# MoBA attention and GELU MLP on one core: batch 0's k sums and gate as fp32 matmuls, the last output row in two pieces, a new order of all steps

## Chip, core and metric

The kernel runs on one core of a Trainium2 chip. A core has five engines with instruction streams of their own: TensorE (PE, matrix products and transposes; its weight loads run beside them as PEld), VectorE (DVE), ScalarE (ACT), GpSimd (POOL) and SyncE (SP, which here only issues DMAs). Sixteen DMA engines move data between HBM and the on-chip memory SBUF. Matrix products write to PSUM, which this kernel uses as eight banks of 512 fp32 columns. The metric is device time in microseconds for one launch, lower is better; the median over several runs counts.

## Reference

q, k and v have the shape (4, 8, 768, 64): 4 batches, 8 heads, 768 tokens, 64 values each. Each token attends causally to its own block of 64 keys and to the three blocks of highest gate score, where a gate score is the product of a query with the mean of the keys of a block. The result, with the heads side by side, is a matrix of 3072 tokens by 512, which goes through an MLP with tanh-GELU (512 to 2048 to 512). All inputs and the output are float32.

```python
    k_rep = k.reshape(B, H, n_blocks, block, D).mean(axis=3)
    gate_scores = np.einsum('bhsd,bhnd->bhsn', q, k_rep)
    ...
    top_idx = np.argsort(gate_scores, axis=-1)[..., -top_k:]
    ...
    mask = mask & (pos[:, None] >= pos[None, :])
    scores = np.where(mask, scores, -1000000000.0)
    ...
    return np.matmul(attn, v).astype(np.float32)
...
    h = x @ w_in
    c = np.float32(np.sqrt(2.0 / np.pi))
    g = 0.5 * h * (1.0 + np.tanh(c * (h + 0.044715 * h * h * h)))
    return (g @ w_out).astype(np.float32)
```

## The kernel before

Nothing is scheduled by the compiler: the kernel gives each small piece of work a name, a step, and a long string ORDER lists all 1113 steps in program order. An engine executes its own instructions in that order and waits on semaphores only for data and for buffers. A step's name ends with `@0`, `@1` or `@2` where it takes one of the three wide PSUM buffers (two banks each), and with `:a`, `:v` or `:p` where it can run on ACT, DVE or POOL. One further PSUM bank belongs to the pool `small` (gates, mask transposes, x transposes, the k sums of later batches) and one to the pool `ops` (results of the down projection, and the filler).

The work has three parts.

*Batch 0* is done in slices, so that something can start before much is loaded. A unit g.c is a group g of four heads and a slice c of 256 tokens; there are six. The letters of its steps: d0 and dd load (L348 to L383), r re-sorts a loaded slice in SBUF (L385), t2 transposes q and k in fp32 on PE into a wide buffer w (L426), h2 makes the fp16 version, scaled by 32 (L445), l the fp16 remainder of q, "low part" (L452), s the sums of k over blocks of 64 (L461), b puts them into the block matrix kb0 as high and low part (L471), v copies v to fp16 (L488), g computes the gate as four fp16 products, high and low part of each side (L495), m selects (L512), mt and mc turn the mask (L542, L551), k computes scores (L565), ma adds the mask on PE (L582), x is the exponential (L603), a the causal cut on POOL (L622), p the product with v (L631), n the normalisation (L646), xt and xc the transposition of the result into xT, the MLP's input (L663, L673).

*Batches 1 to 3* are done in pairs of heads, p = 4 to 15, four pairs for a batch. d loads (L397), hn and ln make high and low fp16 parts (L706, L713), zqh, zkh and zql transpose them by DMA (L723, issued by SP), c0 and c1 copy them into the score operands (L733), and s, b, g, m, mt, mc, k (six bins), x, a, p, n, xt and xc follow as above (L738 to L877).

*The MLP* is done in 12 chunks of 256 tokens. u.ch.dj.half is the up projection, 8 matmuls of 256 columns (L913); dj counts quarters of the 2048 hidden values. y is the GELU of a quarter (L930). f.ch.ti.dj is a quarter of the down projection for 128 tokens, 4 matmuls of 512 columns into an `ops` bank (L938); o copies that bank to SBUF (L950), w stores it (L955). The weights come in eight pieces of 512 KB each for w_in and w_out, loaded by lw (L319) and cast to fp16 by cw (L331).

The constants are steps too (c.*). The steps dmN issue N matmuls of zeros by zeros (L970), whose result nobody reads. All loads go through SP's queue in the order of the list, except that `load_first` issues the k parts from ACT (L356). The SBUF pools that matter: io has 9 buffers for loaded q, k and v, w32 has 7 for raw weights, otp has 2 for output rows.

```python
        dma = nc.scalar if x == 1 else nc.sync
...
    def k_sum0(g, c):
        ks = hd.tile([128, 2, 4], FP32, tag="ks", name=f"ks_{g}_{c}")
...
    for name in ORDER.split():
        do(name)
```

Of the kernel before, what the change touches and what calls it, by code (L numbers as in the profile page):

```python
# [26 lines left out]
d0.0.0.0 d0.0.1.0 d0.0.0.1 c.bd c.e0 c.ident d0.0.1.1 c.e.3:p c.gate dd.0.1.0 dd.0.1.1 d0.1.1.0  # L27
d0.1.0.0 c.e.2:v d0.1.0.1 r.0.1.0:p dm20 t2.0.0@0 r.0.1.1:p d0.1.1.1 c.m0.0 dd.1.1.0 d0.0.1.2
c.m0.1 c.ident16 h2.0.0 s.0.0 dm14 t2.0.1@1 h2.0.1 b.0.0 dd.1.1.1 l.0.0 s.0.1 g.0.0 c.own t2.1.0@2
h2.1.0 lw.in.5 d0.1.1.2 m.0.0 s.1.0 c.e.1:p dm9 mt.0.0 l.1.0 r.1.1.0:a mc.0.0:a b.1.0 r.1.1.1:p  # L30
# [4 lines left out]
p.0.0.3 dd.0.2.1 lw.in.4 d0.1.3.2 p.0.0.2 dm3 k.0.1.1.1@1 a.1.0.0 mc.0.1:a a.1.0.1 ma.0.1.1 b.1.1
v.1.0.0:p cw.in.5:p r.0.2.0:p lw.in.7 v.1.0.1:a n.0.0 lw.in.1 g.1.1 r.0.2.1:p x.0.1.0.1 x.0.1.1.1
r.1.2.0:p cw.in.4:p dm7 k.0.1.0.0@0 k.0.1.1.0@2 ma.0.1.0 m.1.1 t2.0.2@1 x.0.1.0.0 s.0.2 dm11
mt.1.1 p.1.0.0@0 p.1.0.2 p.1.0.3 x.0.1.1.0 p.1.0.1 dd.1.2.1 d0.0.2.2 n.1.0 mc.1.1:a k.1.1.1.1@2
# [986 lines left out]
```

## Time and profile before

| | |
|---|---|
| median of 3 runs (280.5 to 281.12) | 280.53 us |
| span of the profiled execution | 278.3 us |
| granted TensorE clock, mean | 0.994 |
| matmul instructions | 2910 |
| down projection, 384 of 128x512 (L944) | 95.0 us busy |
| up projection, 768 of 128x256 (L923) | 92.9 us busy |
| exponentials of pairs, 72 (L845) | 62.9 us of ACT |
| GELU, 48 (L933) | 47.8 us of ACT |
| HBM read, written | 27.26 MB, 6.29 MB |

The span goes from the first to the last instruction of one profiled execution; the runs are timed without the profiler, and their median lies 2.2 us above that span. An engine's busy time counts only instructions that compute; a slice digit in the profile's picture is the busy share of a fortieth of the span in tenths. A group of instructions is written as line, engine, operation, output<-input, size, number, then busy time, mean nanoseconds of one, and the idle time ahead of it with what ended most of that. The chain of waits starts at the last instruction and goes back, at each step to what released it.

### The profile page before, as it was taken

The page shows a single profiled execution, that of the slowest core. Times are in us where ns is not written, and L with a number is a line of the kernel's source. Part 1 is how long each engine was busy: PE and PEld are TensorE (multiplying, and loading weights), DVE is VectorE, ACT ScalarE, POOL GpSimd, SP SyncE. Part 2 cuts the span into 40 slices and gives each one's busy share as a digit, 9 for nine tenths or more (in the row PEclk, how much of TensorE's full clock was granted, in tenths as well). Part 3 has the DMA queues.
Part 4 walks back from the last instruction along what each step waited for, and adds up shares of the span by engine and source line. Part 5 has one row for each costly group of instructions (what it writes and reads, how often), then busy time and mean ns, then how long its engine had stood idle before and what let it go on. Part 6 is the DMA issues. An engine that isn't in the chain of part 4 may idle for free.

```text
span 278.3 us, 7163 instructions
## 1 busy us (share of the span) xinstructions
PE 264.5 (95%) x2910; PEld 188.8 (68%) x2910; DVE 139.3 (50%) x431; ACT 192.8 (69%) x221; POOL 131.4 (47%) x193
## 2 busy tenths in 40 slices
PE   5899697999999999999999999999999999999994
PEld 5677583865787666886766756786676777756651
DVE  2697458786878686867376466553442010000000
ACT  1568487788699979958898876897887753412330
POOL 6447699899725488870825929400352200000000
PEclk9999799999999999999999999999999999999999
DMA  8998999999699887998998984803112101010102
GB/s 177 272 258 266 346 287 225 245 263 183 110 207 220 181 172 145 204 237 110 169 228 194 245 132 101 166 2 59 39 38 77 40 0 40 38 40 0 75 0 113
DMA packets 107872, 41.09 MB, mean 148 GB/s; under 512 B 96576, under 2 KB 100672, under 8 KB 107840
## 3 DMA queue, kind: packets, MB, share of 16 engines
q1 hardware_dynamic: 105728, 40.12, 65.6%
q10 hardware_dynamic: 2112, 0.52, 1.0%
q8 instruction: 22, 0.36, 0.6%
q14 instruction: 10, 0.08, 0.1%
HBM read 27.26 MB, written 6.29 MB: 121 GB/s over the span
## 4 chain that ended last, share of the span: by engine, by line
PE 84%; DVE 4%; ACT 4%; DMA 3%; POOL 3%; issue 1%; ACTq 0%; DVEq 0%; POOLq 0%
PE ops L944 28%; PE hps L923 28%; PE st L829 9%; PE pv L871 6%; DMA w_in<-in_moe_w_in_dram 3%; PE st L576 2%; PE pv L640 2%; PE dm L976 2%; PE xt L667 1%; PE w L442 1%; ACT qk L448 1%; PE mt L807 1%; PE gt L771 1%; PE kp L742 1%; PE st L594 1%
## 5 line engine op out<-in xcount | busy, mean ns | idle before, releaser
L944 PE MATMUL ops<-w_out,gT 128*128 128x512 f16 x384 | 95.0, 379 | 0.7 <-ACT osb L952 0.7
L923 PE MATMUL hps<-xT,w_in 128*128 128x256 f16 x768 | 92.9, 275 | 0.0
L923 PEld LDWEIGHTS <-w_in 128*128 128x128 f16 x768 | 74.6, 99 | 14.9 <-issue 0.2
L845 ACT ACTIVATE at<-st 128x1024 f16<-128x1024 f32 (+1 forms) x72 | 62.9, 918 | 12.7 <-PE st L829 11.1
L933 ACT ACTIVATE gT<-hps 128x1024 f16<-128x1024 f32 x48 | 47.8, 1024 | 27.8 <-PE hps L923 27.4
L859 POOL TENSOR_SCALAR_AFFINE_SELECT at<-at 128x256 f16<-128x256 f16 x72 | 31.2, 449 | 59.8 <-ACT at L845 57.1
L944 PEld LDWEIGHTS <-gT 128*128 128x128 f16 x384 | 35.7, 97 | 33.4 <-issue 1.9
L184 POOL TENSOR_SCALAR hn<-io 128x768 f16<-128x768 f32 x15 | 34.3, 2284 | 8.6 <-DMA io<-in_q_dram 6.4
L829 PE MATMUL st<-qk 76*128 76x128 f16 (+2 forms) x192 | 36.1, 305 | 0.6 <-ACT at L845 0.5
L952 DVE COPY osb<-ops 128x512 f32<-128x512 f32 x11 | 7.6, 690 | 50.5 <-PE ops L944 47.5
L716 DVE SCALAR_TENSOR_TENSOR ln<-io,hn 128x768 f16<-128x768 f32 x24 | 24.1, 1005 | 1.8 <-POOL hn L184 1.5
L613 ACT ACTIVATE at<-st 128x768 f16<-128x768 f32 (+1 forms) x24 | 20.7, 915 | 6.2 <-PE st L594 6.2
L829 PEld LDWEIGHTS <-qk 76*128 76x128 f16 x192 | 16.6, 97 | 11.8 <-issue 1.1
L871 PEld LDWEIGHTS <-at 128*128 128x128 f16 x504 | 17.4, 97 | 1.8
L871 PE MATMUL pv<-v,at 128*128 128x65 f16 x504 | 18.1, 193 | 0.0
L952 ACT COPY osb<-ops 128x512 f32<-128x512 f32 x13 | 7.6, 585 | 12.3 <-PE ops L944 12.0
L976 PE MATMUL dm<-zsrc 128*128 128x128 f16 x144 | 11.5, 233 | 3.2 <-POOL zsrc L230 3.2
L933 ACT ACT_TABLE_LOAD x11 | 14.1, 1283 | 0.2
L651 DVE RECIPROCAL zrec<-pv 128x12 f32<-128x12 f32 x12 | 2.8, 231 | 19.3 <-PE pv L871 19.1
L976 PEld LDWEIGHTS <-zsrc 128*128 128x128 f16 x144 | 9.6, 105 | 3.9 <-POOL zsrc L230 3.1
L448 ACT ACTIVATE qk<-w 128x1024 f16<-128x1024 f32 x6 | 6.2, 1029 | 8.2 <-DVE ks L464 4.3
L735 POOL COPY qk<-khT 64x768 f16<-64x768 f16 x14 | 11.5, 820 | 0.6
(136 smaller groups left out, 320.4 us busy)
## 6 DMA issues: line engine op xcount, KB each, us to landing
out_dram<-osb SPq DMA_DIRECT2D x24, 256.0 KB, 2.3
io<-in_q_dram SPq DMA_DIRECT2D x24, 192.0 KB, 4.3
io<-in_k_dram SPq DMA_DIRECT2D x24, 192.0 KB, 3.9
io<-in_v_dram SPq DMA_DIRECT2D x24, 192.0 KB, 3.8
w_in<-in_moe_w_in_dram SPq DMA_DIRECT2D x8, 512.0 KB, 6.6
w_out<-in_moe_w_out_dram SPq DMA_DIRECT2D x8, 512.0 KB, 6.6
io<-in_v_dram SPq DMA_DIRECT2D x12, 128.0 KB, 5.3
io<-in_q_dram SPq DMA_DIRECT2D x4, 256.0 KB, 4.9
```

What stands on the lines that cost most here:

```text
L184: math_on[eng].tensor_scalar(out=out, in0=in_, scalar1=c, scalar2=None, op0=ALU.mult)
L613: nc.scalar.activation(out=ov, in_=iv, func=AF.Exp, bias=0.0, scale=SCALE / (QS * QS))
L716: math_on[eng].scalar_tensor_tensor(out=g.rearrange("p t c -> p (t c)"), in0=IO[p, x].rearrange("p t h d -> p (t h d)"), scalar=QS, in1=U[ ...
L829: nc.tensor.matmul(st[:, hh, cb:cb + nq * 128], kt[p % 2][hh][0:64 + NBLK, jc * 128:(jc + 1) * 128], qt[p % 2][hh][0:64 + NBLK, qc * 128:( ...
L845: nc.scalar.activation(out=ov, in_=iv, func=AF.Exp, bias=0.0, scale=SCALE / (QS * QS))
L859: nc.gpsimd.affine_select(out=a, in_=a, compare_op=ALU.is_ge, fill=0.0, base=0, pattern=[[0, 2], [1, 128]], channel_multiplier=-1,)
L871: nc.tensor.matmul(U["pv", p][:, o:o + 65], AT[p, hh, jc, qc], v16[p % NSLOT][:, jc, hh, :], start=(jc == 0), stop=(jc == qc),)
L923: nc.tensor.matmul(hps[:, j * TCH:(j + 1) * TCH], w_in16[:, ci, fi * 128:(fi + 1) * 128], xT[:, ci, t0:t0 + TCH], start=(ci == 0), stop=(c ...
L933: nc.scalar.activation(out=g.rearrange("p a w -> p (a w)"), in_=G["h", ch, dj], func=AF.Gelu_apprx_tanh, bias=0.0, scale=1.0,)
L944: nc.tensor.matmul(G["o", ch, ti], G["g", ch, dj][:, j, ti * 128:(ti + 1) * 128], w_out16[:, fi, :], start=(fi == 0), stop=(fi == NF - 1),)
L952: copy_on[eng](out=osb, in_=G["o", ch, ti])
L976: nc.tensor.matmul(U["dm"][:, 0:128], zsrc, zsrc, start=True, stop=True)
```

## The change

- **Order.** The whole list is replaced (1109 steps). Steps stand elsewhere, wide buffers and engines are assigned anew. The filler shrinks from fifteen dm steps with 144 matmuls of 128 columns to dm3 and dm9, issued as 4 matmuls of up to 512 columns. The last chunk of 12 is still last, but chunk 10's rows end before chunk 9's.
- **k sums of batch 0.** `k_sum0` no longer reduces the transposed k on DVE. It multiplies the untransposed fp32 k on PE with an indicator matrix of the blocks (ind32, made by the new step c.ind): four fp32 matmuls for each unit, 24 in all, into an `ops` bank. `k_block0` writes the fp32 block matrix with one operation in place of three.
- **Gate of batch 0.** `q_full` copies the transposed fp32 q to SBUF, into a loaded tile that is no longer needed, where `q_low` made the low part. `gate0` is one fp32 matmul for each 128 tokens and pair of heads, 20 in all, in place of 80 fp16 ones.
- **h2** is two steps, for q and for k, each on an engine that the list names; it was one ACT operation.
- **Loads.** `load_first` issues k from SP as well. v of pairs 8 to 15 goes to a w32 buffer.
- **x of pairs 12 to 15** is transposed by DMA straight into xT (step zx, issued by SP) in place of xt on PE and xc.
- **Output.** Output rows of odd ti from chunk 3 on use w32 buffers. The second rows of the last three chunks accumulate in the `small` bank. The last row of chunk 11 is done in two column pieces, 0 to 384 and 384 to 512, each with its own matmuls, copy and store (steps f, o and w of 11.1 and 11.2).

```diff
--- before
+++ after
-d0.0.0.0 d0.0.1.0 d0.0.0.1 c.bd c.e0 c.ident d0.0.1.1 c.e.3:p c.gate dd.0.1.0 dd.0.1.1 d0.1.1.0
-d0.1.0.0 c.e.2:v d0.1.0.1 r.0.1.0:p dm20 t2.0.0@0 r.0.1.1:p d0.1.1.1 c.m0.0 dd.1.1.0 d0.0.1.2
...
-y.11.0 w.9.1 u.11.3.0@1 f.10.0.3 u.11.1.0@0 u.11.1.1 u.11.3.1 o.10.0:v f.11.0.0 y.11.2 y.11.1
-f.11.0.1 f.11.0.2 y.11.3 f.11.0.3 o.11.0:a w.11.0 f.11.1.0 w.10.0 f.11.1.1 f.11.1.2 f.11.1.3
-o.11.1:a w.11.1
+c.ident c.ind dd.0.1.0 r.0.1.0:a c.ident16 d0.0.1.0 c.bd c.v.0 c.gate c.par.0 c.m0.1 c.e0 dm3
+d0.0.1.2 d0.1.0.0 d0.0.0.0 d0.0.0.1 d0.0.1.1 t2.0.0@0 h2.0.0.0:v d0.1.1.0 d0.1.1.1 c.bi c.e.1:a
...
+xc.1.0:v v.0.1.1:p h2.0.2.0:a h2.0.2.1:a l.0.2:a ma.1.1.1 b.0.2 x.1.1.0.1 lw.in.0 x.1.1.1.1
+u.0.2.0@1 u.0.2.1 cw.in.0:v v.0.1.0:a g.0.2 t2.1.2@0 u.0.0.0@2 u.0.0.1 cw.out.1:v y.0.2 lw.in.2
+cw.in.2:p y.0.0 u.0.1.0@1 u.0.1.1 lw.out.3 a.0.1.1 h2.1.2.0:v a.0.1.0 y.0.1 m.0.2 lw.out.0
...
+f.11.1.0 f.11.1.1 f.11.0.0 f.11.0.1 y.11.2 f.11.0.2 f.11.0.3 w.5.1 o.11.0:a f.11.1.2 f.11.1.3
+f.11.2.0 f.11.2.1 w.9.1 w.11.0 o.11.1:a w.11.1 f.11.2.2 f.11.2.3 o.11.2:a w.11.2
...
+    P32 = 8
+    C32 = 3
+    XDMA = 12
 
...
+    ind32 = const.tile([128, 6], FP32)
...
-    kb0 = [persist.tile([128, 2, 4, NBLK], FP16, name=f"kb0_{g}")
+    kb0 = [persist.tile([128, 4, NBLK], FP32, name=f"kb0_{g}")
            for g in range(NG)]
...
+    def c_ind():
+        nc.vector.tensor_reduce(
+            out=ind32[:, 0:2], in_=ident32.rearrange("p (n w) -> p n w", w=64),
+            axis=AXL.X, op=ALU.add)
+        nc.vector.tensor_reduce(
+            out=ind32[:, 2:6], in_=ident32.rearrange("p (n w) -> p n w", w=32),
+            axis=AXL.X, op=ALU.add)
+
...
+    step("c.ind", c_ind)
...
-        dma = nc.scalar if x == 1 else nc.sync
+        dma = nc.sync
...
     def load(p, x):
         b, hp = divmod(p, HP)
-        a = io.tile([128, NC, 2, D], FP32, tag="io", name=f"io_{p}_{x}")
+        if x == 2 and p >= P32:
+            a = w32p.tile([128, 2, 512], FP32, tag="w32", name=f"w32_v_{p}")
+            a = a.rearrange("p a x -> p (a x)")[:, 0:NC * 2 * D].rearrange(
+                "p (t h d) -> p t h d", h=2, d=D)
+        else:
+            a = io.tile([128, NC, 2, D], FP32, tag="io", name=f"io_{p}_{x}")
...
+    def hi(g, c, x, eng):
+
+        h = qk[g][:, c * 1024:(c + 1) * 1024].rearrange(
+            "d (j x t) -> d j x t", j=2, x=2)
+        w = U["w", g, c].rearrange("d (j x t) -> d j x t", j=2, x=2)
+        scaled(eng, h[:, :, x], w[:, :, x], QS)
         U["h", g, c] = h
 
-    def q_low(g, c):
-        ql = hd.tile([128, 2, 256], FP16, tag="ql", name=f"ql0_{g}_{c}")
+    def q_full(g, c, eng):
+
         w = U["w", g, c].rearrange("d (j x) -> d j x", j=2)
-        nc.vector.scalar_tensor_tensor(
-            out=ql, in0=w[:, :, 0:256], scalar=QS,
-            in1=U["h", g, c][:, :, 0], op0=ALU.mult, op1=ALU.subtract,
-        )
-        U["ql", g, c] = ql
+        if c == 0:
+            q32 = IO["first", g, 1][:, 0]
+            w = w[:, :, 128:256]
+        else:
+            q32 = IO["part", g, c][:, 0].rearrange("d (j x) -> d j x", j=2)
+            w = w[:, :, 0:256]
+        copy_on[eng](out=q32, in_=w)
+        U["q32", g, c] = q32
 
     def k_sum0(g, c):
-        ks = hd.tile([128, 2, 4], FP32, tag="ks", name=f"ks_{g}_{c}")
-        w = U["w", g, c].rearrange("d (j x) -> d j x", j=2)
-        nc.vector.tensor_reduce(
-            out=ks, in_=w[:, :, 256:512].rearrange("d j (n w) -> d j n w",
-                                                   w=64),
-            axis=AXL.X, op=ALU.add,
-        )
+        t = opsp.tile([128, 512], FP32, tag="ops", name=f"ks_{g}_{c}")
+        ks = t[:, 0:8].rearrange("p (j n) -> p j n", j=2)
+        for j in range(2):
+            for y in range(2):
+                if c == 0:
+                    nc.tensor.matmul(ks[:, j, 2 * y:2 * y + 2],
+                                     IO["first", g, y][:, 1, j], ind32[:, 0:2],
+                                     start=True, stop=True)
+                else:
+                    nc.tensor.matmul(
+                        ks[:, j],
+                        IO["part", g, c][:, 1, y * 256 + j * 128:
+                                         y * 256 + (j + 1) * 128],
+                        ind32[:, 2:6], start=y == 0, stop=y == 1)
         U["ks", g, c] = ks
 
     def k_block0(g, c):
         b0 = 4 * c
-        kbd = hd.tile([128, 2, 2, 4], FP32, tag="kbd", name=f"kbd0_{g}_{c}")
         nc.vector.tensor_tensor(
-            out=kbd,
+            out=kb0[g].rearrange("d (j h) n -> d j h n", j=2)[
+                :, :, :, b0:b0 + 4],
             in0=U["ks", g, c].unsqueeze(2).to_broadcast([128, 2, 2, 4]),
             in1=bdmask[:, :, 0:4].unsqueeze(1).to_broadcast([128, 2, 2, 4]),
             op=ALU.mult,
-        )
-        kbd = kbd.rearrange("d j h n -> d (j h) n")
-        kh = kb0[g][:, 0, :, b0:b0 + 4]
-        nc.vector.tensor_copy(out=kh, in_=kbd)
-        nc.vector.scalar_tensor_tensor(
-            out=kb0[g][:, 1, :, b0:b0 + 4], in0=kh, scalar=-1.0, in1=kbd,
-            op0=ALU.mult, op1=ALU.add,
         )
 
     def v_copy0(g, c, y, eng):
...
         gt = small.tile([128, 512], FP32, tag="small", name=f"gt0_{g}_{c}")
         ta = max(2 * c, 1)
         for n, t in enumerate(range(ta, 2 * c + 2)):
-            cs = slice((t - 2 * c) * 128, (t - 2 * c + 1) * 128)
+            a = (t - max(2 * c, ta)) * 128
             for j in range(2):
-                src = (U["h", g, c][:, j, 0], U["ql", g, c][:, j])
-                for i in range(4):
-                    nc.tensor.matmul(
-                        gt[:, (2 * n + j) * 24:(2 * n + j + 1) * 24],
-                        src[i // 2][:, cs],
-                        kb0[g][:, i % 2, 2 * j:2 * j + 2].rearrange(
-                            "d h n -> d (h n)"),
-                        start=i == 0, stop=i == 3)
+                nc.tensor.matmul(
+                    gt[:, (2 * n + j) * 24:(2 * n + j + 1) * 24],
+                    U["q32", g, c][:, j, a:a + 128],
+                    kb0[g][:, 2 * j:2 * j + 2].rearrange("d h n -> d (h n)"),
+                    start=True, stop=True)
         U["gt", g, c] = gt
 
     def select0(g, c):
...
             op=ALU.mult,
         )
         U["xn", *key] = xn
+        U["xn", key[0]] = xn
 
     def x_t(key, nt, un):
         t = small.tile([128, 512], FP32, tag="small", name=f"xt_{un}")
...
         for g in range(NG):
             un = f"{g}.{c}"
             step(f"t2.{un}", t_in, g, c)
-            step(f"h2.{un}", hi, g, c)
-            step(f"l.{un}", q_low, g, c)
+            for x in range(2):
+                step(f"h2.{un}.{x}", hi, g, c, x)
+            step(f"l.{un}", q_full, g, c)
             step(f"s.{un}", k_sum0, g, c)
             step(f"b.{un}", k_block0, g, c)
             for y in range(2):
...
                     v16[p % NSLOT][:, jc, hh, :],
                     start=(jc == 0), stop=(jc == qc),
                 )
+
+    def x_dma(p):
+
+        b, hp = divmod(p, HP)
+        nc.sync.dma_start_transpose(
+            out=xT[:, hp, b * S:(b + 1) * S].rearrange(
+                "d (t p) -> d t p", p=128),
+            in_=U["xn", p].rearrange("p t h d -> p (t h d)"))
 
     def x_c(p, eng):
         b, hp = divmod(p, HP)
...
         for hh in range(2):
             step(f"p.{un}.{hh}", pv, p, hh)
         step(f"n.{un}", normalise, (p,), NC, p)
-        step(f"xt.{un}", x_t, (p,), NC, p)
-        step(f"xc.{un}", x_c, p)
+        if p < XDMA:
+            step(f"xt.{un}", x_t, (p,), NC, p)
+            step(f"xc.{un}", x_c, p)
+        else:
+            step(f"zx.{un}", x_dma, p)
 
 
     out_rows = out.rearrange("(n p) c -> n p c", p=128)
...
             func=AF.Gelu_apprx_tanh, bias=0.0, scale=1.0,
         )
 
+    LAST = NCH - 1
+    CUT = 384
+
+    def columns(ch, ti):
+
+        if ch < LAST or ti == 0:
+            return ti, 0, DM
+        return (1, 0, CUT) if ti == 1 else (1, CUT, DM)
+
     def down(ch, ti, dj):
-        if dj == 0:
-            G["o", ch, ti] = opsp.tile([128, 512], FP32, tag="ops",
-                                       name=f"ops_{ch}_{ti}")
+        row, a, b = columns(ch, ti)
+        if dj == 0 and row == ti:
+            if ch >= LAST - 2 and ti == 1:
+                o = small.tile([128, 512], FP32, tag="small",
+                               name=f"pso_{ch}_{ti}")
+            else:
+                o = opsp.tile([128, 512], FP32, tag="ops",
+                              name=f"ops_{ch}_{ti}")
+            G["o", ch, ti] = o
         for j in range(4):
             fi = 4 * dj + j
             nc.tensor.matmul(
-                G["o", ch, ti],
-                G["g", ch, dj][:, j, ti * 128:(ti + 1) * 128],
-                w_out16[:, fi, :], start=(fi == 0), stop=(fi == NF - 1),
+                G["o", ch, row][:, a:b],
+                G["g", ch, dj][:, j, row * 128:(row + 1) * 128],
+                w_out16[:, fi, a:b], start=(fi == 0), stop=(fi == NF - 1),
             )
 
     def out_c(ch, ti, eng):
-        osb = otp.tile([128, DM], FP32, tag="osb", name=f"osb_{ch}_{ti}")
-        copy_on[eng](out=osb, in_=G["o", ch, ti])
+        row, a, b = columns(ch, ti)
+        if ch >= C32 and ti % 2:
+            osb = w32p.tile([128, 2, 512], FP32, tag="w32",
+                            name=f"w32_o_{ch}_{ti}")[:, 0]
+        else:
+            osb = otp.tile([128, DM], FP32, tag="osb", name=f"osb_{ch}_{ti}")
+        copy_on[eng](out=osb[:, a:b], in_=G["o", ch, row][:, a:b])
         G["s", ch, ti] = osb
 
     def out_d(ch, ti):
-        nc.sync.dma_start(out=out_rows[ch * (TCH // 128) + ti],
-                          in_=G["s", ch, ti])
+        row, a, b = columns(ch, ti)
+        nc.sync.dma_start(out=out_rows[ch * (TCH // 128) + row][:, a:b],
+                          in_=G["s", ch, ti][:, a:b])
 
     for ch in range(NCH):
         for dj in range(4):
             step(f"u.{ch}.{dj}.0", up, ch, dj, 0)
             step(f"u.{ch}.{dj}.1", up, ch, dj, 1)
             step(f"y.{ch}.{dj}", gelu, ch, dj)
-        for ti in range(TCH // 128):
+        for ti in range(TCH // 128 + (ch == LAST)):
             for dj in range(4):
                 step(f"f.{ch}.{ti}.{dj}", down, ch, ti, dj)
             step(f"o.{ch}.{ti}", out_c, ch, ti)
             step(f"w.{ch}.{ti}", out_d, ch, ti)
 
+    dms = []
+
     def idle(n):
 
 
-        if "dm" not in U:
-            U["dm"] = opsp.tile([128, 512], FP32, tag="ops", name="dm")
-        for _ in range(n):
-            nc.tensor.matmul(U["dm"][:, 0:128], zsrc, zsrc, start=True,
-                             stop=True)
+        dm = opsp.tile([128, 512], FP32, tag="ops", name=f"dm_{len(dms)}")
+        dms.append(dm)
+        while n > 0:
+            m = min(n, 4)
+            nc.tensor.matmul(
+                dm[:, 0:m * 128].rearrange("p (a x) -> p a x", a=m), zsrc,
+                zsrc.unsqueeze(1).to_broadcast([128, m, 128]), start=True,
+                stop=True)
+            n -= m
 
     def do(name):
         if name.startswith("dm"):
```

More of the change, by code (lines that the diff above doesn't have):

```diff
@@ L129 @@
+f.10.1.2 f.10.1.3 o.10.1:a u.11.0.0@1 u.11.0.1 u.9.2.0@2 u.9.2.1 y.9.2 f.10.0.2 f.10.0.3 o.10.0:v
+w.10.0 w.10.1 u.11.3.0@0 w.6.1 u.11.1.0@2 u.11.3.1 y.11.3 f.9.0.0 f.9.0.1 f.9.0.2 f.9.0.3 o.9.0:v
+f.9.1.0 f.9.1.1 w.9.0 w.8.1 y.11.0 u.11.1.1 f.9.1.2 f.9.1.3 o.9.1:a y.11.1 u.11.2.0@0 u.11.2.1
+f.11.1.0 f.11.1.1 f.11.0.0 f.11.0.1 y.11.2 f.11.0.2 f.11.0.3 w.5.1 o.11.0:a f.11.1.2 f.11.1.3
+f.11.2.0 f.11.2.1 w.9.1 w.11.0 o.11.1:a w.11.1 f.11.2.2 f.11.2.3 o.11.2:a w.11.2
 """
```

192 lines of the change are left out of this document (91 added, 101 removed).

## Prediction

> **What bounds the kernel now.** I read the page's totals and slices first, then busy time in stretches of 10 us, then the chain of waits, then the timeline of single engines at the places that the chain names.
>
> ```profile
> span 278.3 us, 7163 instructions
> PE 264.5 (95%) x2910; PEld 188.8 (68%) x2910; DVE 139.3 (50%) x431; ACT 192.8 (69%) x221; POOL 131.4 (47%) x193
> ...
> PE   5899697999999999999999999999999999999994
> ...
> DMA  8998999999699887998998984803112101010102
> ```
> ```profile
> 0.00:10.00 10.00, 6.26 (x52) 5.54 (x52) 3.15 (x11) 3.02 (x3) 6.65 (x21) 1.00 0.95 197
> 20.00:30.00 10.00, 8.76 (x155) 6.78 (x154) 7.39 (x25) 8.15 (x13) 6.09 (x9) 1.00 0.88 265
> 30.00:40.00 10.00, 8.89 (x86) 7.00 (x87) 4.42 (x19) 5.64 (x6) 8.71 (x12) 0.83 1.06 307
> 40.00:50.00 10.00, 8.39 (x140) 5.29 (x138) 7.97 (x22) 7.62 (x9) 9.77 (x8) 1.00 1.02 235
> 50.00:60.00 10.00, 10.00 (x164) 8.29 (x161) 8.10 (x27) 8.71 (x10) 8.90 (x10) 1.00 1.06 274
> 80.00:100.00 20.00, 19.91 (x242) 13.66 (x239) 14.70 (x51) 18.82 (x21) 10.54 (x16) 1.00 1.07 205
> ```
> The columns of the stretches are PE, PEld, DVE, ACT, POOL busy time, granted clock, DMA share, GB/s. There are two regimes. From 50 us on PE has no free time (10.00 of 10): there only less PE work, or a wait at the end, changes the time. Before 50 us PE is busy too, but partly with filler, and the DMA engines are full (share about 1).
>
> ```profile
> L976 PE MATMUL dm<-zsrc 128*128 128x128 f16 x144 | 11.5, 233 | 3.2 <-POOL zsrc L230 3.2
> ```
> ```profile
> 26.74 8.33 DMA w_in<-in_moe_w_in_dram
> 35.12 1.04 POOL w_in L337
> ...
> 37.45 1.28 POOL at L626 x2
> 38.74 2.12 POOL hn L184
> ...
> 40.88 1.77 DVE ln L716
> ...
> 42.80 0.70 DVE xn_0.1_957 L655
> ...
> 50.51 0.98 PE hps L923 x8
> ```
> The filler (dm) is 11.5 us. The chain of waits (start, length, what) says what ends the first regime: the load of the last piece of w_in for chunk 0 (lw.in.2, landed at 35.07), its cast on POOL, two causal masks queued behind it, an hn of pair 4 on POOL (2.12), its ln on DVE (1.77), and only then the normalisation xn of unit 0.1 on DVE, which PE waits for. At 50.51 chunk 1's up projection (u.1.0) begins, and PE never idles long again.
>
> So time = start of the full regime + PE work left + overhead. The work left goes by count times rate, from merged rows of the chain:
> ```profile
> 53.78 3.50 PE hps L923 x32
> 60.76 0.28 PE mt L807 x5
> 61.91 0.97 PE ops L944 x4
> 71.42 0.23 PE xt_0.2_1581 L667 x4
> 77.75 0.28 PE kp L742 x12
> 79.80 0.25 PE gt L771 x10
> 81.78 1.29 PE pv L871 x42
> 241.87 3.45 PE ops L944 x16
> ```
> An up matmul is 0.109, a down one 0.216, a PV one 0.031, a transpose 0.056 to 0.058 us. I take f.0.0.3 as the mark, which starts at 61.91 and needs the last piece of w_out. From there the order of before still holds 656 up (71.8), 372 down (80.2), the scores of 12 pairs with 5,376 columns each at 0.109 us per 256 (27.6), 504 PV (15.5), 10 k sums (2.8), 11 gates (2.8), 11 mask transposes (3.1), 72 x transposes (4.1), batch 0's rest (2.5): 210.3. 278.3 - 61.91 - 210.3 = 6.1 us is overhead, most of it at the end:
> ```profile
> 270.53 0.59 ACT osb L952
> ...
> 271.17 3.63 PE ops L944 x16
> ...
> 274.86 0.59 ACT osb L952
> ```
> 0.64 us in which PE waits for the copy that frees the one ops buffer, and 3.4 us from the last copy's start to the end; 2.0 us are scattered.
>
> **The change part by part.**
>
> *PE work from f.0.0.3 on.* 24 x transposes go (pairs 12 to 15, now by DMA): -1.4. The last row's 16 matmuls of 512 columns become 16 of 384 and 16 of 128: 3.50 for 3.45 by columns. By place in the new order there are 0.3 more mask transposes and 0.2 less of batch 0 after the mark. Sum 209.0.
>
> *The end.* The last copy has a quarter of the columns: between 0.15 and 0.59 us, taken as 0.3, as part of a copy is fixed. The 0.64 us wait leaves o.11.0, but the built program's last 128-column matmuls wait for ACT, so the copy of the first piece: about the same again. Overhead 5.8 instead of 6.1.
>
> *The x transposes by DMA.*
> ```profile
> L655 DVE TENSOR_TENSOR xn<-pv,zrec 128x768 f16<-128x768 f32 x12 | 11.5, 958 | 0.4
> ```
> ```profile
> qlT<-ln SPq DMA_TRANSPOSE x12, 3.7
> ```
> zx.15 follows n.15, whose product takes 0.96 us; a transpose of the same size lands 3.7 us after its issue (median), on fuller DMA engines. From the last PV to u.10.2, the first reader of batch 3, PE has 24 up and 16 down matmuls, 6.1 us, so 1 us is spare and I cost it at nothing. Without that work it would cost 4.7. The new homes of the v loads of pairs 8 to 15 and of half the output tiles (the w32 buffers, idle after the weights) cost nothing either: PE waits for neither.
>
> *Batch 0's sums and gate.* Removed from DVE: 6 reduces, 6 low parts, and two of three kb operations.
> ```profile
> L464 DVE TENSOR_REDUCE ks<-w 128x8 f32<-128x512 f32 x6 | 4.1, 691 | 6.4 <-ACT qk L448 4.2 <-PE w L442 2.0
> L442 PE MATMUL w<-ident,w_q 128*128 128x128 f32 x32 | 5.1, 297 | 2.4 <-POOL w_q L390 2.4
> ```
> ```profile
> 5.26 1.92 PE L442 MATMUL w<-ident,io 128*128 128x128 f32 x8
> 32.02 3.94 PE L923 MATMUL hps<-xT,w_in 128*128 128x256 f16 x24
> ```
> ```profile
> 24.28 1.02 PE w L442 x8
> ```
> PE loses 80 fp16 gate matmuls (2.0 us at 0.025) and gains 24 fp32 sums and 20 fp32 gates. No fp32 product is in the trace. The nearest row is the fp32 transpose, with the same weight size: 0.128 us each in a stream, 0.297 alone. 44 of them are 5.6 to 13.1 us; I take 0.2, 8.8 us, since each runs in short groups of two and four. They lie in the first 46 us, where 11.5 us of filler went away, so they are hidden unless PE itself fills up (third rival). On the Trainium skill's page "FP8 and Floating Point Precision", TensorE Precision Notes, a true fp32 product takes four passes; by that, four times the transpose, 0.51 each and 22.5 us, PE would be short of time here, and no row here shows it.
>
> All sums go through the one ops buffer: each unit's sum waits until DVE's kb operation has read the one before, with all of PE queued behind. That is one short DVE operation, put in the order well ahead, in the first regime: nothing, or some tenths.
>
> q_full stands for the low part, and hi comes in two halves. With all that moved between engines, ACT has 12 operations more and six shorter by half; at the 0.59 us of an osb copy that is 4 to 6 us more ACT work. POOL loses five hn (2.12 in the chain) and six casts (1.04): 17 us.
>
> *The first loads.* Seven instead of four DMAs come before t2.0.0, all on SP; the 512 KB more are 2.7 us at the first stretch's 197 GB/s, so PE's first transposes start near 8 instead of 5.26. This is hidden: what follows waits for weights.
>
> *The filler* shrinks from 144 matmuls to 4 wide ones. It computes nothing, but keeps PE's clock up: the first 8 fp32 transposes took 1.92, later ones 1.02; the ups at 32.02 took 3.94 for 24 (0.164 each, not 0.109), in the stretch with clock 0.83, right after PE had stood idle for want of k data. This speaks against the change: up to 0.055 us on each of chunk 0's 48 ups, 2.6 us. I take half, 1.3, which the forecast of u.0.1 below holds. The Trainium skill ("TensorE: Matmul & The Clock Gate", Part 1) has the rule: after about 3.4 us without enough work the clock falls to half. By it all PE work before 46 us could run at half speed, which the third rival prices from the rows above.
>
> *The new order, up to the full regime.* In SP's order lw.in.2 ends at 7,680 KB instead of 8,576. At the 307 GB/s of its stretch the 896 KB less are 3.0 us: it lands at 32.1, is cast by 33.2. Then u.0.1 (1.75, with the slow clock 2.4) ends at 35.5 and its GELU starts.
> ```profile
> 39.02 1.02 ACT L933 ACTIVATE gT<-hps 128x1024 f16<-128x1024 f32 x1 [0.43 <-PE hps L923]
> 40.06 1.28 ACT L613 ACT_TABLE_LOAD   x1
> 47.39 1.94 ACT L613 ACTIVATE at<-st 128x1024 f16<-128x1024 f32 x2 [0.39 <-PE st L594]
> ```
> Before, this GELU starts at 39.02, 11.5 us ahead of u.1.0. Now ACT has that GELU (1.02), a table load (1.28), six exponentials (1.02 each) and one xc copy (0.6) before u.1.1 gets its PSUM slot: 9.0 us without a gap, and the hn on POOL that stood in the chain is now on DVE, behind n.0.1. 35.5 + 9.0 to 11.5 is 44.5 to 47; I take 45.5 for u.1.1. Between it and f.0.0.3 lie 13.0 us of PE work (64 ups 7.0, eight down 1.7, scores with masks of unit 1.2 2.1, PV 0.2 1.35, the k sums and a gate 0.85): 58.5.
>
> *The last w_out piece.*
> ```profile
> 59.79 1.04 POOL L337 CAST w_out<-w_out 128x1024 f16<-128x1024 f32 x1
> ```
> Its cast ended at 60.83 and stood in POOL's queue, not behind a DMA. It has 128 KB less ahead of it now (0.5 us at 274 GB/s), so at worst 60.3; POOL is freer, so earlier. f.0.0.3 starts between 58.5 and 60.3: I take 59.0, 2.9 us earlier than before.
>
> **Sum:** 59.0 + 209.0 + 5.8 = 273.8 us of span. The runs' median is 280.53 with a profiled span of 278.3, so 2.2 are added: 276.0.
>
> **Rivals.**
> - *The whole head start stays.* u.1.1 starts at 43.5, with u.0.1 at full clock and 8 us of ACT behind it, and the w_out pieces come 3 us earlier too. For it: POOL's load is 24 us less. Against: DMA share is 1.06 in 50 to 60 us, with nearly the same bytes ahead. 56.5 + 209.0 + 5.8 + 2.2 = 273.5.
> - *The gain is handed back later.* ACT is busy 18.82 of 20 us at 80 to 100 us, and it gets 4 to 6 us more work. If all of that falls where ACT has only the 1.2 us to spare, PE waits 3 to 5 us there: around 280.3, about as before. Against: the new order changes between exp and GELU, each with a table load, no more often than the old, and much of ACT's new work is batch 0's.
> - *PE becomes the bound of the first regime; slower.* Place: before u.1.1. PE's other work there is 23 us by the rates above (48 transposes 6, 48 ups 5, batch 0's attention 12); 44 fp32 products at 0.297 are 13.1; start at 8. That is 44 with no wait at all. If the 23 us run at the slow rates of above (1.5 to 1.9 times) for half their length, 6 to 10 us come on top, and some waits: u.1.1 at 53, so 53 + 13.0 + 209.0 + 5.8 + 2.2 = 283.0. It decides from u.1.1 at 50.5 on, where the sum is as before. For it: filler gone, unknown price of fp32. Against: a slow PE is a fuller PE, and the stretch at 0.83 shows that the clock comes back within a few us.
> - *The tail does not get shorter*, as the wait for the first piece's copy takes the place of the old one: 0.3 us more than forecast, inside the range.
>
> **How the numbers follow.** The forecast, with the tail's rival in it, has 0.52, the whole head start 0.14, handed back 0.20, the PE-bound start 0.14. Less than 0.3% (0.84 us) can't be told from no change here. Faster: 0.52 + 0.14 = 0.66. Handed back is half within the bound and half beyond it: same 0.10, slower 0.10 + 0.14 = 0.24. The range goes from 1 us below the second case, 272.5, to the PE-bound start, 283.5; the forecast's own range is 274 to 279.
>
> **What would show it.** In the profile after: lw.in.2's cast near 33, u.1.1 near 45.5, f.0.0.3 near 59, PE busy 10 of 10 from there; fp32 sums at 0.2 each; clock under 1.00 somewhere before 40 us; no PE wait ahead of u.10.2; a copy of about 0.3 at the end. The forecast is wrong if u.1.1 comes after 50.5, or PE has more than 2 us of waits between 60 and 270 us.

## The result: 3.7% slower, and where it came from

The changed kernel takes 291.5 us (median of 4 runs, 290.33 to 292.65) beside 280.82 (280.5 to 282.16): 1.0374 times as long, 95% interval 1.0328 to 1.042. The forecast was 276.0, and the time lies 8 us above its range. The profiled execution took 290.33, with a span of 288.5. Of the kernels in the table below, one execution of four of old_fp32 and two of four of old_sums were in a slower state: the ratios leave them out and the medians don't, so for these two the ratio counts.

The head of its page:

```profile
span 288.5 us, 6865 instructions
PE 274.0 (95%) x2770; PEld 197.8 (69%) x2770; DVE 132.6 (46%) x424; ACT 198.6 (69%) x233; POOL 110.8 (38%) x175
...
PE   1998999899999999999999999999999999999995
...
PEclk9999999999999999999999999999999999999999
```

PE is as busy as before, and the row of the granted clock shows no fall. Filler of 11.5 us went, yet PE has 9.5 us more busy time. The stretches of the first 60 us (columns as before) say where:

```profile
0.00:10.00 10.00, 3.69 (x17) 3.11 (x18) 2.36 (x8) 2.73 (x3) 6.60 (x27) 1.00 0.81 186
10.00:20.00 10.00, 10.00 (x60) 9.36 (x61) 3.48 (x16) 5.08 (x12) 0.40 (x1) 1.00 1.12 308
20.00:30.00 10.00, 8.67 (x65) 6.78 (x68) 5.18 (x23) 3.13 (x5) 3.56 (x8) 1.00 0.48 125
30.00:40.00 10.00, 10.00 (x85) 7.93 (x81) 4.25 (x18) 5.95 (x9) 4.62 (x7) 1.00 0.77 234
40.00:50.00 10.00, 10.00 (x116) 8.88 (x118) 6.33 (x21) 6.25 (x8) 4.05 (x6) 1.00 1.07 246
```

From 10 us on PE is nearly full, but with few instructions: 60 in 10 us, where before there were 155 in the stretch from 20 to 30. They are long. From PE's timeline of the changed kernel (start, length, what, number):

```profile
8.61 1.71 PE L488 MATMUL ks<-ind,io 128*128 128x2 f32 x8
10.18 1.95 PE L459 MATMUL w<-ident,io 128*128 128x128 f32 x8
...
36.54 1.95 PE L459 MATMUL w<-ident,w_q 128*128 128x128 f32 x8
...
40.37 2.35 PE L954 MATMUL hps<-xT,w_in 128*128 128x256 f16 x16
42.56 0.97 PE L523 MATMUL gt<-kb,w_q 128*128 128x24 f32 x8
43.37 1.07 PE L459 MATMUL w<-ident,w_q 128*128 128x128 f32 x8
...
48.20 1.03 PE L492 MATMUL ks<-ind,w_q 128*128 128x4 f32 x8
...
58.71 5.40 PE L954 MATMUL hps<-xT,w_in 128*128 128x256 f16 x48
...
72.41 1.02 PE L990 MATMUL ops<-w_out,gT 128*128 128x512 f16 x4
```

The same eight transposes take 1.95 us up to 36.5 and 1.07 at 43.4: up to the first up projection (40.37) PE runs at about half its rate. And an fp32 product shows as two records, so that "x8" are four products: 0.39 us each at the low rate (8.61 to 10.18), 0.22 at the high one (48.20 to 49.09). Chunk 1 (u.1.1) starts at 58.71, where the forecast had 45.5, and f.0.0.3 at 72.41 instead of 59.0. From there to the end it is 216.1 us; before it was 216.4 from 61.91. So all of the loss, and nearly all of the forecast's error, lies before the mark.

### The profile page after: what moved, and what is told of

The parts are those of the page before. It is cut to its first block, busy times and chain, and to the rows that moved or that the text cites. A ratio compares the mean times of both kernels' runs of the same rounds, so it can differ in the third digit from the quotient of the medians.

```text
span 288.5 us, 6865 instructions
## 1 busy us (share of the span) xinstructions
PE 274.0 (95%) x2770; PEld 197.8 (69%) x2770; DVE 132.6 (46%) x424; ACT 198.6 (69%) x233; POOL 110.8 (38%) x175
## 4 chain that ended last, share of the span: by engine, by line
PE 85%; ACT 4%; DVE 4%; POOL 2%; issue 2%; DMA 1%; SPq 1%; ACTq 0%; POOLq 0%
PE hps L954 27%; PE ops L990 22%; PE st L849 8%; PE pv L891 5%; PE pso L990 4%; PE w L459 4%; PE st L594 3%; PE gt L523 2%; PE ks L492 2%; ACT at L631 2%; PE st L612 2%; POOL hn L186 1%; PE kp L762 1%; DMA io<-in_q_dram 1%; PE ks L488 1%
## 5 line engine op out<-in xcount | busy, mean ns | idle before, releaser
L954 PE MATMUL hps<-xT,w_in 128*128 128x256 f16 x768 | 89.9, 273 | 0.0
L990 PE MATMUL ops<-w_out,gT 128*128 128x512 f16 x336 | 80.8, 379 | 0.0
L849 PE MATMUL st<-qk 76*128 76x512 f16 (+2 forms) x192 | 35.7, 305 | 0.7 <-ACT qk L836 0.3
L186 POOL TENSOR_SCALAR hn<-io 128x768 f16<-128x768 f32 x10 | 22.1, 2213 | 1.5 <-DMA io<-in_k_dram 0.8
L644 POOL TENSOR_SCALAR_AFFINE_SELECT at<-at 128x512 f16<-128x512 f16 x12 | 9.5, 800 | 17.9 <-ACT at L631 17.9
L1003 DVE COPY osb<-ops 128x512 f32<-128x512 f32 x7 | 4.8, 689 | 19.0 <-PE ops L990 19.0
L755 POOL COPY qk<-qhT 64x768 f16<-64x768 f16 x14 | 12.4, 888 | 2.1 <-PE st L849 1.1
L836 DVE COPY qk<-mt 12x640 f16<-12x640 f16 x17 | 8.2, 484 | 10.6 <-ACT qk L836 6.4
L990 PE MATMUL pso<-w_out,gT 128*128 128x512 f16 (+2 forms) x64 | 11.4, 326 | 0.6 <-ACT w_o L1003 0.6
L673 DVE TENSOR_TENSOR xn<-pv,zrec 128x768 f16<-128x768 f32 x12 | 11.5, 957 | 0.4
```

The lines of the kernel that those rows point to most:

```text
L186: math_on[eng].tensor_scalar(out=out, in0=in_, scalar1=c, scalar2=None, op0=ALU.mult)
L755: copy_on[eng](out=dst[0:64, :], in_=U["qh" if x == 0 else "kh", p][64 * hh:64 * hh + 64])
L849: nc.tensor.matmul(st[:, hh, cb:cb + nq * 128], kt[p % 2][hh][0:64 + NBLK, jc * 128:(jc + 1) * 128], qt[p % 2][hh][0:64 + NBLK, qc * 128:( ...
L954: nc.tensor.matmul(hps[:, j * TCH:(j + 1) * TCH], w_in16[:, ci, fi * 128:(fi + 1) * 128], xT[:, ci, t0:t0 + TCH], start=(ci == 0), stop=(c ...
L990: nc.tensor.matmul(G["o", ch, row][:, a:b], G["g", ch, dj][:, j, row * 128:(row + 1) * 128], w_out16[:, fi, a:b], start=(fi == 0), stop=(f ...
```

## The experiments

Three theories stood at the start. Clock: PE runs at about half its rate because the filler is gone. Price: the fp32 products themselves take too long. Order: in the new list SP's queue waits for w32 buffers, whatever PE does. Names that begin with new_, and head_fill and all_fill, are variants of the changed kernel; names that begin with old_ are variants of the one before. Each run was timed beside the kernel before on the same chip; ratios are against that. "Ups" is the start of chunk 1's first up projection in the profile (58.71 in the changed kernel, 51.62 before). Filler is counted in columns-of-128: dm8 is eight of them, issued as two matmuls of 512 columns.

| kernel | median us | ratio (95%) | ups | span |
|---|---|---|---|---|
| new_fp16 | 287.68 | 1.0228 (1.0188 to 1.0268) | 56.58 | 286.8 |
| head_fill | 290.0 | 1.0323 (1.028 to 1.0367) | 59.68 | 289.5 |
| all_fill | 286.5 | 1.0209 (1.0165 to 1.0253) | 54.40 | 284.3 |
| new_fp16_fill | 287.1 | 1.0218 (1.0162 to 1.0273) | 57.05 | 287.2 |
| new_cheap | 280.88 | 0.9973 (0.9953 to 0.9993) | 48.79 | 278.9 |
| new_cheap_fill | 280.72 | 0.9973 (0.9944 to 1.0001) | 49.95 | 279.6 |
| old_nofill | 282.58 | 1.0037 (1.0003 to 1.0072) | 54.39 | 281.4 |
| old_fp32 | 286.06 | 1.0152 (1.0082 to 1.0221) | 58.28 | 285.9 |
| old_fp32_nofill | 289.02 | 1.0264 (1.0222 to 1.0306) | 59.16 | 285.9 |
| old_sums | 286.47 | 1.0112 (1.0039 to 1.0184) | 56.68 | 283.9 |
| old_tail | 281.93 | 1.0018 (0.9987 to 1.0048) | 53.33 | 278.9 |
| old_best | 279.05 | 0.9923 (0.9895 to 0.9951) | 51.98 | 277.6 |

In the new order span less ups is 229.6 to 230.2 in every row (229.8 in the changed kernel). So these kernels differ only ahead of chunk 1. Several expectations below take the two records of an fp32 product for two products (four sums in 0.4 us, 44 x 0.21 or x 0.117); the price of one product is twice that.

**The filler in the new order.**

```diff
-dm3
+dm56
```

> The changed kernel with 56 filler columns-of-128 (14 wide matmuls) instead of 3 ahead of the first transposes, nothing else. Clock theory, strong form (PE runs at half its rate until it has once been dense, and then stays up as long as it is busy): the eight transposes of t2.0.0 and all later ones take about 0.9 to 1.0 us instead of 1.81, chunk 1's first up starts near 47 instead of 58.7, time 279 to 282. Clock theory, weak form (the short fp32 sums and gates do not keep the rate up): fast until some 10 to 13 us, then 1.8 us for eight transposes again, time 288 to 291. Price theory (the fp32 products themselves take the time): 291. Order theory (SP's queue waits for w32 buffers in the new order): 291.

290.0 fits the weak form, but lies near the 291 of the other two theories too; the trace decides. PE's timeline of head_fill:

```profile
8.26 0.95 PE L490 MATMUL ks<-ind,io 128*128 128x2 f32 x8
9.07 1.10 PE L461 MATMUL w<-ident,io 128*128 128x128 f32 x8
12.30 1.05 PE L525 MATMUL gt<-kb,io 128*128 128x24 f32 x4 [2.13 <-ACT io L481]
13.18 1.84 PE L490 MATMUL ks<-ind,io 128*128 128x2 f32 x8
14.89 1.95 PE L461 MATMUL w<-ident,w_q 128*128 128x128 f32 x8
```

With a dense head the sums take 0.95 at once. After one wait of 2.13 us (for ACT's copy of q) the same step takes 1.84, and the rate stays low to the ups, although PE idles only 1.3 us from 15 to 40. So these short products and transposes, near full as they keep PE, didn't bring the rate back.

```diff
+dm10 g.0.0
...
+dm12 s.1.0
...
+dm8 u.0.2.0
```

> The changed kernel with the same 56 at the head and 13 further fillers of 8 to 12 between the steps of batch 0, some 125 x 128 columns more. Clock theory, either form: eight transposes at 0.9 to 1.0 us throughout, four fp32 sums at about 0.4, chunk 1's first up at 45 to 48, time 277 to 281. Price theory: PE only gets more to do, 291 to 299. Order theory: about 290.

286.5: the rate stays high up to 47 us (transposes 1.07 at 37.55), and chunk 1 comes 4.3 us earlier, at 54.40, but not at 45 to 48. Behind a wait of 1.14 us at 47 the rate falls for some 3 us (28 PV matmuls 1.73 at 49.26, 1.02 in the changed kernel). The 116 columns-of-128 of filler behind the head take 6.3 us of PE (0.43 for eight of them, by the starts) in a stretch where PE is full, so by these two numbers the higher rate bought some 10 us and the filler gave 6 back. The price theory, which had 291 or more here, is not enough by itself.

**Filler and fp32 in the old order.**

```diff
-r.0.1.0:p dm20 t2.0.0@0 r.0.1.1:p
+r.0.1.0:p t2.0.0@0 r.0.1.1:p
```

(and likewise for the 14 other dm steps)

> The kernel before with its 144 filler matmuls left out, fp16 gates and DVE sums as they were. Clock theory: eight transposes take 1.8 us up to the ups, as in the changed kernel; the 23 us of other PE work ahead of chunk 1 grow by 5 to 10, time 284 to 290. Price theory and order theory: the filler was outside the chain of waits, so 280 to 281, or a few tenths less.

282.58, below what the clock theory expected: by the ratio 0.4% more, 1 us. Its rate is mostly low, as foreseen, up to some 28 us, and costs little; it is back up ahead of chunk 0's ups (four transposes in 0.61 at 30.12):

```profile
25.48 1.97 PE L442 MATMUL w<-ident,w_q 128*128 128x128 f32 x8
...
54.39 1.91 PE L923 MATMUL hps<-xT,w_in 128*128 128x256 f16 x16
```

With fp16 gates, sums on DVE and no filler, PE has gaps that absorb slow transposes. So in the old order the low rate alone doesn't cost the time.

```diff
-h2.0.0 s.0.0 dm14 t2.0.1@1 h2.0.1 b.0.0
+h2.0.0.0:a h2.0.0.1:a s.0.0 b.0.0 dm14 t2.0.1@1 h2.0.1.0:a h2.0.1.1:a
...
-    kb0 = [persist.tile([128, 2, 4, NBLK], FP16, name=f"kb0_{g}")
+    kb0 = [persist.tile([128, 4, NBLK], FP32, name=f"kb0_{g}")
```

(sums, block step, copied q and gates as in the change; each b step right behind its s)

> The kernel before, its order, its filler and its end, with the fp32 k sums on PE, the one-operation block step, the copied fp32 q and the fp32 gates put in. Clock theory: with the rate up four sums take 0.4 to 0.45 us, 44 products 4.5 to 5 us in place of 2.0, hidden by the filler: 280 to 283. Price theory: 286 to 291. Order theory: 280 to 281.

By the ratio 1.5% more (0.8 to 2.2), 4.3 us, so 285.2 beside 280.95: above the clock theory's 283 and just below the price theory's 286. Filler is no slack that products could slip into: it is issued in order whether or not there is room, so the products lengthen PE's queue wherever PE doesn't wait. There is clock in it too. PE's first sums, behind the slow first transposes, take 1.71. And the rate falls twice with PE busy all the time and, since the first transposes, no wait over 0.27 us ahead, each time behind k sums (granted clock 0.53 from 16.9 to 19.3 and 0.56 from 25.5 to 29.4). 16 filler matmuls there take 1.79 us, in the kernel before 1.07 (old_fp32 first):

```profile
17.61 1.79 PE L1031 MATMUL dm<-zsrc 128*128 128x128 f16 x16
```
```profile
18.64 1.07 PE L976 MATMUL dm<-zsrc 128*128 128x128 f16 x16
```

```diff
-r.0.1.0:p dm20 t2.0.0@0
+r.0.1.0:p t2.0.0@0
```

(and the 14 others, in old_fp32)

> old_fp32 without its 144 fillers. Theory now: the filler's 11.5 us go, but the rate stays low up to the ups as in old_nofill, so that transposes and products cost about twice as much; PE stays full and chunk 1's first up comes at 54 to 58, time 285 to 289. If old_fp32 lost its time to the filler's own place in PE's queue: 281 to 283.

289.02, at the top of what the joint theory expected; its ups, at 59.16, come later than 54 to 58. Without filler the products cost 6.4 us in the old order (282.58 to 289.02), with it 4.3 by the ratio; the intervals are too wide to tell the two apart.

```diff
-        ks = hd.tile([128, 2, 4], FP32, tag="ks", name=f"ks_{g}_{c}")
+        t = opsp.tile([128, 512], FP32, tag="ops", name=f"ks_{g}_{c}")
+        ks = t[:, 0:8].rearrange("p (j n) -> p j n", j=2)
...
-        nc.vector.tensor_reduce(
+                    nc.tensor.matmul(ks[:, j, 2 * y:2 * y + 2],
```

> The kernel before with only the k sums moved to fp32 matmuls on PE (24 products); low parts, block step with three operations and fp16 gates stay. Theory now: 24 of the 44 products, 24 x 0.12 to 0.2 = 2.9 to 4.8 us more PE work in a stretch where filler is issued whether or not PE has room, plus six waits of 0.27 for the one ops bank: 283 to 285. Clock theory: 281 to 282. If the gates were the dear part: 281 to 282.

1.1% more (0.4 to 1.8), some 3 us, as the joint theory had it: the 24 sums alone seem to cost more than half of the 4.3 us of all 44 products, but the two intervals overlap.

**Back to fp16 in the new order.**

```diff
-    step(f"l.{un}", q_full, g, c)
+    step(f"l.{un}", q_low, g, c)
```

(with the old k_sum0, k_block0 and gate0)

> The changed kernel, its order and its small filler, but with the old sums (DVE reduces of the transposed k, set right behind the transposes), low parts and fp16 gates of batch 0. Theory now (the product of two: 44 fp32 products of 0.2 us each because the rate is low, on a PE that has no room for them): about 7 us less PE work ahead of chunk 1, whose first up then starts at 50 to 53; 280 to 285. Clock alone (the low rate costs the time whatever runs): 288 to 291. Order (SP waits for w32 buffers in the new order whatever PE does): 288 to 291.

> The same as new_fp16, with the 181 fillers of all_fill. Theory now: rate up and no fp32 products, chunk 1's first up at 47 to 50, 278 to 282. Clock alone: as all_fill, 285 to 287. Order: 286 to 290.

Both missed: 287.68 and 287.1. PE's waits in new_fp16 up to 48 us (what waited, for what, us, times, longest) say why:

```profile
PE gt L523 <- DVE kb L501: 2.4, 1, 2.4
PE st L595 <- DVE ql L474: 2.0, 2, 1.2
PE mt L565 <- DVE madd L552: 1.8, 1, 1.8
PE w L460 <- DVE kbd L493: 1.5, 1, 1.5
```

The new order has moved h2, casts and copies to DVE; with the reduces and low parts put back, PE waits 7.7 us for DVE in these four rows. In new_fp16_fill the rate wasn't up as expected either: eight columns-of-128 of filler take 0.99 us at 14.95, by the starts, where all_fill has 0.43. This doesn't separate the theories, so the products were made cheap without touching any other engine.

```diff
-                                     IO["first", g, y][:, 1, j], ind32[:, 0:2],
+                                     top(IO["first", g, y][:, 1, j]),
+                                     top(ind32)[:, 0:2],
```

(top() is the upper half of each fp32 number, read as bf16; likewise in the other sums and in the gates)

> The changed kernel with the same 44 sums and gates in the same places, their operands read as bf16 (the upper half of each fp32 number), so that each is one short product; the gates are therefore less exact and other blocks may be selected. Theory now (fp32 products at the low rate fill a PE that has no room): 44 x (0.21 - 0.03) = 8 us less PE work ahead of chunk 1, its first up at 50 to 52, time 282 to 285. Clock alone: 288 to 291. Order (SP's waits): 288 to 291.

280.88, even below the joint theory's 282: the whole loss is gone, in the same order, with the same small filler and the same dependencies between steps. Groups of the changed kernel first (number of records; busy us, mean ns), then of new_cheap:

```profile
L492 PE MATMUL ks<-ind,w_q 128*128 128x4 f32 x32 | 6.5, 326 | 0.0
L523 PE MATMUL gt<-kb,w_q 128*128 128x24 f32 x32 | 5.8, 327 | 0.0
L488 PE MATMUL ks<-ind,io 128*128 128x2 f32 x16 | 3.6, 344 | 0.0
L523 PE MATMUL gt<-kb,io 128*128 128x24 f32 x8 | 1.9, 372 | 0.0
```
```profile
L500 PE MATMUL ks<-ind,w_q 128*128 128x4 bf16 x16 | 1.1, 173 | 0.0
L531 PE MATMUL gt<-kb,w_q 128*128 128x24 bf16 x16 | 1.1, 181 | 0.0
L495 PE MATMUL ks<-ind,io 128*128 128x2 bf16 x8 | 0.5, 171 | 0.0
L531 PE MATMUL gt<-kb,io 128*128 128x24 bf16 x4 | 0.5, 191 | 1.0 <-ACT io L479 1.0
```

17.8 us of PE for 44 fp32 products, 3.2 for 44 bf16 ones. The rate of new_cheap is as low as the changed kernel's, to 29 us at least:

```profile
27.43 1.95 PE L459 MATMUL w<-ident,w_q 128*128 128x128 f32 x8
...
48.79 5.40 PE L963 MATMUL hps<-xT,w_in 128*128 128x256 f16 x48
```

The order theory (SP's waits by themselves) falls as well. SP's longest wait for a w32 buffer was 8.6 us in the changed kernel; it is 3.5 here. An exponential, a causal mask and the last cast of w_in for chunk 0, in the changed kernel; then the cast in new_cheap:

```profile
26.86 1.51 ACT L631 ACTIVATE at<-st 128x768 f16<-128x768 f32 x2 [6.21 <-PE st L612]
28.44 0.64 POOL L644 TENSOR_SCALAR_AFFINE_SELECT at<-at 128x512 f16<-128x512 f16 x1 [5.72 <-ACT at L631]
39.41 1.04 POOL L349 CAST w_in<-w_in 128x1024 f16<-128x1024 f32 x1 [2.81 <-DMA w_in<-in_moe_w_in_dram]
```
```profile
32.38 1.04 POOL L349 CAST w_in<-w_in 128x1024 f16<-128x1024 f32 x1 [2.35 <-DMA w_in<-in_moe_w_in_dram]
```

Slow PE makes scores late, then the exponentials (a wait of 6.21 us), then the causal masks on POOL (5.72), behind which the casts stand that free SP's w32 buffers. In new_cheap the same two waits are 2.76 and 2.26 us. The loads are late because PE is.

> The same bf16 operands in all_fill. Theory now: with the rate up the products save 44 x (0.117 - 0.03) = 3.8 us against all_fill, chunk 1's first up at 50 to 51, time 282 to 284. Clock alone or order: 285 to 288.

280.72, also below what was expected. With cheap products filler gains nothing (ups at 49.95 against 48.79); with fp32 products it gained 5.0 us. In the new order the products cost 10.6 us without filler (291.5 to 280.88) and 5.8 with it (286.5 to 280.72); by the ratios, as the kernel before ran some 0.6 us longer beside the bf16 runs, 11.3 and 6.6. So here the price of a product and the low rate act together: cheap products remove the loss, the high rate about half of it.

**The other parts.**

```diff
+    XDMA = (12, 13, 14)
...
+        if p not in XDMA:
             step(f"xt.{un}", x_t, (p,), NC, p)
             step(f"xc.{un}", x_c, p)
+        else:
+            step(f"zx.{un}", x_dma, p)
...
+        return (1, 0, CUT) if ti == 1 else (1, CUT, DM)
...
+            if ch >= LAST and ti == 1:
+                o = small.tile([128, 512], FP32, tag="small",
```

> The kernel before with two parts of the change alone: x of pairs 12 to 14 transposed by DMA (18 PE transposes less, 1.0 us), and the last row in the small bank and in two pieces, the second of them in the ops bank, so that no matmul waits for a copy (0.64 us less, and a last copy of 128 columns in place of 512, 0.3 us less). Both count in full: 278.6 to 279.3. If the DMA transposes come late: 281 to 284.

No difference that can be told. Its part from f.0.0.3 on is 215.35 us (216.46 before), so 1.1 of the expected 1.9 is there; the start covers it, with ups at 53.33 in this profile and at 51.62 in that of before. In old_tail's profile the rate fell behind a wait of 1.07 us: the 28 PV matmuls, 1.03 in the profile of the kernel before, took 1.72.

```profile
44.04 0.85 PE L578 MATMUL st<-qk 64*128 64x256 f16 x8 [1.07 <-DVE xn_0.1_957 L657]
...
45.37 1.72 PE L642 MATMUL pv<-v,at 128*128 128x65 f16 x28
```

```diff
+dm32 t2.1.2@1
...
 f.0.0.0
+dg4
```

(old_tail with these; dg4 writes four products of zeros to unused columns of gt_1.2's bank)

> old_tail with two more fillers: 32 columns-of-128 ahead of t2.1.2, whose second half waits some 2 us for data, and four of 384 columns behind f.0.0.0, where PE waits 1.1 us, into unused columns of the gate's bank. Theory: the rate no longer falls at these two places, as it did in some executions of the kernel before and of old_tail; together with the shorter end 278.5 to 280. If the falls have another cause: 281 to 282.

279.05, 0.8% less than before (0.5 to 1.1): the fastest of all. The mean granted clock is 1.0 in 10 of its 12 executions (0.986 to 0.994 in old_tail's), and in the profile the rate holds behind the wait:

```profile
42.31 0.81 PE L1016 MATMUL gt<-zsrc 128*128 128x384 f16 x4
...
44.42 1.03 PE L642 MATMUL pv<-v,at 128*128 128x65 f16 x28
```

That the rate is what made it faster isn't shown: of the kernel before, timed beside it, four of 28 executions have a mean clock of 1.0 too, and they take 280.99 to 281.86, in the midst of the others (280.73 to 283.37).

## Why the prediction was wrong

**The step that failed** is "They lie in the first 46 us, where 11.5 us of filler went away, so they are hidden unless PE itself fills up", together with the clock term of 1.3 us. PE did fill up: it is busy 32.86 of the 34.2 us from 6.8 to 41. The forecast had 8.8 us of products and a penalty on 48 ups. Measured were 17.8 us of products, as the 0.2 taken for each holds only at the high rate and most of them ran at the low one, and 40 fp32 transposes up to 38 us at nearly twice their price (1.95 for 1.07 in eight), some 4 us more. The removal of the filler was counted once, as room gained; that it also halves the rate of all that stays was costed only where the trace of before showed a clock below 1.00.

**The third rival** (PE bound from the start, 283.0, chance 0.14) names the mechanism that runs showed, with both of its conditions. Its sizes were short: 13.1 us of products against 17.8, half of the other work at slow rates against nearly all of it, chunk 1 at 53 against 58.71. What the prediction held against it, that the clock comes back within a few us, failed: the rate stayed low for some 34 us. It deserved the place of the forecast: its own sum had PE busy to 44 of 50 us before any slow rate was counted.

**lw.in.2** was not cast by 33.2 but by 40.5. The forecast went by bytes in SP's order and left out that SP waits for w32 buffers, which hang on PE through POOL. In new_cheap, where PE isn't the bound, the same cast ends at 33.4, close to the forecast's 33.2.

**The two rules that the prediction cited.** By the Trainium skill's page "FP8 and Floating Point Precision", TensorE Precision Notes (four passes), the estimate was 22.5 us, which lies above the 17.8 measured, mostly at the low rate, and far above the 9 to 11 that 0.20 to 0.25 each would be at the high one, but nearer to what happened than my 8.8. Of the rule of the Trainium skill's page "TensorE: Matmul & The Clock Gate", Part 1 (half clock without enough work), the halving agrees, 1.95 against 1.07 us for the same transposes, and it spoke against the change as the prediction said. What counts as enough work the busy time doesn't tell: PE was busy 10.00 of 10 us from 10 to 20 us and stayed slow.

**From chunk 1 on** the forecast held: 13.7 us to f.0.0.3 (13.0), then 216.1 (214.8). PE's busy time there fell by 0.7 instead of 1.3 us, 211.5 to 210.8, and a k sum waits 0.7 us for an ln on DVE. The second rival (gain handed back to ACT) had no gain to hand back; PE's waits for ACT after the mark stay below 1.5 us in all. The row at 50.51 that the prediction took for chunk 1 of before is the second half of u.0.3; chunk 1 begins at 51.62 there. The sum ran through f.0.0.3, so nothing hung on it.

**The end** came as forecast. The chain that ended last, changed kernel:

```profile
282.64 1.76 PE pso L990 x16
284.40 0.02 issue
284.42 0.49 ACT w_o L1003
284.91 0.04 issue
284.95 0.62 PE pso L990 x8
285.57 0.02 issue
285.60 0.27 ACT osb L1003
```

A copy of 0.27 us (0.3 forecast), and the 128-column matmuls wait for the copy of the first piece, as in the fourth rival. The transposes by DMA stay hidden: no PE wait ahead of batch 3's ups.

**Without the fp32 price** (new_cheap) the new order gives 280.88, not 276: its ups start at 48.79, 3.3 us behind the forecast. The rate is still low up to 29 us and falls once more at 44 us, but that this holds the ups back isn't shown: in new_cheap_fill the rate is high for most of the time up to 43 us (eight transposes 1.07 at 17.17, 28.96 and 33.78), and the ups come at 49.95, with some 6 us of filler on PE. The cause of these 3.3 us stays open.

## What to carry to other kernels

Before an operation counts as hidden on an engine, add up all that this engine must issue in order up to the due time, at the rate that it will have there; filler is part of that sum, not slack. Filler that comes out can take PE's rate with it, as it did in both orders here, so every product that stays has to be priced at both rates, and the change is safe only if it fits at the lower one. Whether PE is slow is read from the same instruction at two places of the trace, not from its busy share, nor from the granted clock alone.

## What the runs showed of the hardware

- The granted clock reads 1.00 in all stretches of the changed kernel's first 40 us, while PE runs at about half its rate; in head_fill, whose rate first rises and then falls, it reads 0.50 from 15 to 40 us, with the same 1.95 us for eight transposes. A rate that was low from the start doesn't show in these traces' granted clock.
- PE was busy 10.00 of 10 us from 10 to 20 us and the rate didn't rise. What filled it were mostly fp32 products of 2 to 24 columns and fp32 transposes. It rose at 40 to 43 us, while 16 up matmuls ran. Up matmuls aren't needed for that: in new_cheap it rose between 29 and 30 us, ahead of the first ups (an x transpose of four matmuls took 0.61 at 26.22 and 0.40 at 30.13). What raises it stays open.
- An fp32 product of 2 to 24 columns is two records and takes 0.20 to 0.25 us at the high rate, 0.39 to 0.46 at the low one. As bf16 it is one record, and four of them take 0.10 (37.71 to 37.81 in new_cheap).
- The rate fell behind waits of 1 to 2 us (2.13 in head_fill, 1.14 in all_fill, 1.07 in old_tail), but not behind each: the wait of 1.07 us was there before too, that of 1.14 us in the changed kernel at 53 us, and the rate held. Nor is a wait needed: in old_fp32 it fell twice with PE busy throughout.
